# Two PSUM banks emptied by one instruction, merged log sums, factored table fixes and a new order, in a chunked recurrence with an FFT block

## The chip, the cores and the metric

One core of one Trainium2 chip. The metric is the device time of one execution in microseconds (us), as the median of several runs. Every run lists its span on the core and the mean clock that was granted to TensorE (1.0 is full). A run counts as fast when it lies within 1.5% of the fastest run of the same kernel; only fast runs are compared. The engines are called PE (TensorE), DVE (VectorE), ACT (ScalarE) and POOL (GpSimd).

## The reference, cut to what matters

```python
def _attn_ref(r, k, v, w, a, b):            # B, H, S, D = 4, 8, 768, 40, all fp32
    for t in range(S):
        y[:, :, t] = einsum('bhd,bhde->bhe', rt, state)
        Sa = einsum('bhde,bhe->bhd', state, at)
        state = state * wt[:, :, None, :] - einsum('bhd,bhe->bhde', Sa, bt) \
                + einsum('bhd,bhe->bhde', vt, kt)
    return y

def _moe_ref(x, w_ch1, w_ch2):              # x: 4 x 768 x 320
    u = x + np.real(np.fft.fft(np.fft.fft(x, axis=1), axis=2))
    un = (u - mean(u)) / sqrt(var(u) + 1e-6)
    return u + np.maximum(un @ w_ch1, 0.0) @ w_ch2      # 320 -> 1280 -> 320
```

## The kernel before

The recurrence is cut into 24 chunks of 128 steps (6 for each of 4 batches). Each chunk has a part that can be prepared ahead ("prep": running sums of log w on PE, exponentials on ACT, scalings of the inputs, transposes, and three masked products A, N, RV for each head) and a part that needs the state ("chain": several small products, a fourth masked product M, the output y and the new state). After six chunks a batch goes through the Fourier tables, the layer norm and the two dense layers ("post"). For all this there is no scheduler at run time: every operation has a number and one implementation for each engine that may do it, and a long recorded text says in which order, and on which engine, each is issued. The letters are P for PE, A for ACT, D for DVE, G for POOL, S for a DMA and W for a filler matmul that only keeps PE busy.

```python
CODE = "ABC...xyz0123456789+-"
ENGINES = dict(zip("PADGSW", ("PE", "ACT", "DVE", "POOL", "SP", "WARM")))
ORDER = ("AQDASDARDACGBFSBLAAdSAbSAAGATGAHDAUGCZGCaGCbDAcSAgSCeDCgDCpDChDCdDAFDAeS" ...)   # cut
SLOTS = ("ABDCBABCAACBABBAABABCDBFHEAADACAAAFEDABCEFHCFHANLJOIBBBCABBBCAFDEGCHEADG" ...)   # cut: the buffer of each
WIDE = set()
...
    ps = Pool("ps", [psum.tile([128, 512], FP32, tag=f"ps{i}", name=f"ps{i}") for i in range(8)])
...
    op({"DVE": (0.35, lambda: nc.vector.tensor_scalar_mul(nsu16, su16, -1.0))}, w=[NSU], r=[SU])   # the negated mask
```

The product of a chunk for eight heads is written as two halves, even heads in one PSUM bank and odd heads in another. Each half leaves PSUM through a masked eviction: either DVE multiplies by a triangular mask, or ACT copies and then POOL (or DVE) masks in place. `masked` could already do both halves at once, but was not asked to.

```python
    def halves(wide):
        if wide:
            p = PSB(lambda t_: t_.rearrange("p (e q t) -> p e q t", e=2, q=NP), 2)
            return [p], [lambda: p()[:, 0], lambda: p()[:, 1]]
        p2 = [PSB(qv) for _ in range(2)]
        return p2, p2

    def masked(dst, p2, neg=False):
        n_ = 2 // len(p2)                        # 1: a half of 512 columns; 2: both, 1024
        ...
        for e in range(2 // n_):
            o = op({"DVE": (cD(512 * n_), ... nc.vector.tensor_tensor(d_(), all_(p2[e]()), mask, Alu.mult)),
                    "ACT": (cA(512 * n_), ... nc.scalar.activation(d_(), all_(p2[e]()), Act.Copy, scale=...))}, ...)
            op({"POOL": (..., ... nc.gpsimd.affine_select(out=d_(), in_=d_(), compare_op=Alu.is_gt, ...)),
                "DVE": (..., ... nc.vector.tensor_tensor(d_(), d_(), mask2, Alu.mult))}, skip=o, ...)
```

The two other places that the change touches, the sums of the logs and the last fix of the Fourier tables:

```python
        def sums():
            o_ = hd(cum())
            mm(o_, ut16, hi()[:, :, :D], True)
            mm(o_, ut16, low()[:, :, :D], False)
        op({"PE": (cP(2, 320), sums)}, w=[cum["c"]], r=[logw, low, UT], kind="cum")
        if not last:
            def totals():                        # 9 small matmuls into the same bank
                ...
            op({"PE": (0.23, totals)}, w=[cum["t"]], r=[cum["c"], logw, low, ONE, ID, OFF], kind="wl")
...
        def last():
            r_ = DM // 2 - 128
            nc.vector.tensor_scalar_mul(cd[r_:r_ + 1, 3], cd[r_:r_ + 1, 3], 0.5)
            nc.vector.tensor_copy(cd[0:64, 4], cd[0:64, 3])
            nc.vector.tensor_scalar_mul(cd[64:128, 4], cd[64:128, 3], -1.0)
```

Of the kernel before, what the change touches and what calls it, by code (L numbers as in the profile page):

```python
# [12 lines left out]
FP32 = mybir.dt.float32  # L13
# [9 lines left out]
def order_of(text):  # L23
# [6 lines left out]
ORDER = ("AQDASDARDACGBFSBLAAdSAbSAAGATGAHDAUGCZGCaGCbDAcSAgSCeDCgDCpDChDCdDAFDAeSBMGBRPAEDBvSCiAAhABNPCqDCcD"  # L30
    "CfDCsDAiDC-WC-WC-WAnPAoAAfSAjPAmAABGADGBOPAtDBQACrABKSApDB1AAqDE-WE-WEvWAxPAuPAyPArDBISDKSCmDCnDAzA"
    "AsAB2DAIGCoABXAAPGAvPAkPBSAB3PAwDCtDA7PBHSA2PAlAA3ABwSBcPBGSBJSBxSA+DA5DB0SCjGA8AB7PB8AA0PB4PB6AA4D"
    "B5ADQACkDCyPAMGBySBzSA1DBVDFxWBAPBZPBUDCzDA9DBbPC0PEPSC1DD-WDMWC2PDRGAKGDSPBTDClABDABBABEGALDDTPBYP"
    "CuAC3DC8PBdDBaDC4PC5PC6DBWGBePBlPAJGB+GBgPBfDANGC7DDDPC9DBjDDEAAWGB9GCCPCFPBmDBhDDWPBoDDNSDOSDMSDPS"
    "DLSCBGCGPD0PD1PCHDFUSEQSBPADVAD2AEVAB-GCDPC+PCEDFVSDBDDUAD3PD4DCKPCLDC-ADXABqPCPPBrACSDCAGCIPCJDD5P"
    "D6AAVGEWGEXPDbGGXSEUSESSCNDCQDDjPEAPDcAEBADkAD7PD8PD9DERSEYPDaGD+DDePDhPEZABCGDFPEaADAGCUPFaAAZGDZG"
    "DgPDiAAXGCXDAOGD-AAGGDYGBsGCVDECPDGPDHDEdGDdPEbPE5PEHPE6PBtABuGEDDDfDEFDEcAE7ADvPDwAE8PFbGDqPDlPFcP"
    "DyAE9DDtADuGDoDDmDDrDEhAFdAEJPE+PFePE-AEIAGdAEfGFAPEKPEiPFBPFFPELPETSFGAKJSFCDFDDAaDFEAEjPEeGFZSEgG"
    "FXSFgGEMDEkDGeGF8PEmPElPFHPFKDFIDF9PHcSFWSFYSDJGDxGEnAC-WCcWEvPEwDDzGF+AEoPF-PFMPGADEyDCwDEqPFfAEpA"
    "E0PFiDEtDGfPGBPErAFkAEsGFOPGgPGCAFNAGiAGDPFPPGIPGEPHiAGJAFpPGFDGGDE3DFmPFlPFhGFoPFqDGHGFjGFQPGjPFRD"  # L40
    "EOGE1DHBPFrPHjGHCPGZSFnAFtPFuDFwDKPAGaSGnGHgSGYSLJSFsAHDAGKPHEPHFDGPPHkPGcSGhAGkAGmGHoPF3PGNDHGPGLA"
    "F4DGQAF6DHHAHdSFyPHIPF1AHJPHNPHOAHeSHfSHKDGMGDIGGpAGtPGrPGRPGlGGbSFSGHhSHLDHMGF2GFzDGSPGTPGqPKOSKKS"
    "KNSKMSLNSGUDGuPGvDHPPHQDHSDIGPIHPGsAHnAIIAHtAHUPHlPHmAIJPIKDGWGG3PHqGKQGGyPHpAHVAH1PILPHrGLPAHWPG1A"
    "KRPHXPHYPH2DGzDKSPGoAG6DHsGIMAINPKUAIOAG4DHZDHyPGwPGxDKVDG2GKxPIPPISDHwPKyAENGLQGIQDKLSHuAMMSLOSHaG"
    "FTGLRPHzPIUPHvPHxDKbAIVPKTALKSH0ALSPLTAKaAKcSIWPLMSKzPG8PIXDK0DH3PH4DG9DK1PK2AH6AH8PH9DK7PKXGAYGKZG"
    "IbGGVGIfGKWAH-AK8ACvDHbDKePK3PKdPKfAIeDLaANPSLLSCxDKYGLVDIaGIBPICDK4PLUAIEDK5DIgPIhPIjAIlAKgPIiPKhA"
    "KiPK6AG-DInAIoAKjDK9PK+DMSAKnPKqAItPKlDLAAIAGIZGH7GLbGIuDLxPLyPIkGLXGImGLZGLBGIpPIqDIrDLWALYGMTGKsP"
    "LzAIxPLEPL0PKvAKtAI9PLePIsAL1DL2PJDPLdPKoAIyDIvDI5PIzDL3AIwAI+DL4PL5PL6DLFPLfAJEAL9PL+AI0DMOSLgPLhD"
    "JFPI1PJHPJIAJGAL-PMAALGDL7DI2DKuGIYGLnPLiPKpGMNSMPSLcSMQSNRSLoALCPMUPMVPMBGLpGLDAL8GLqAMWAI3DI4AMXA"
    "KrGI6DMCDLjDMGPI7DJbPJLPM0PM1PMHPJXPM2ANQSKwGLlAJMDJcAMYDNVAMZAJYAJJPM3PI-DJZPJAAM4DOQSNUSNSSMIPJTP"  # L50
    "I8AMJDJKDMcGM5PM6AMEPLsPJmPJUDMFDMRSNTSMLGNWGJnAJRPJqPLtDOTSJrALmGJaDJoPNAPNBANXPM7PM8PM9DPTSJpAJVP"
    "NCPMbGMjPLvAJSAORSMkAOWAMaDMhPMgPNFDM+DM-AMdGNYAIcGJWDNDDMiDNZDJuPJ+PN1PMKGJ8POXGJ9AJvAJ-AJ6PN2PN3D"
    "MqPMlPN8PLrGMrAOYPOZPOSSNJPN4PNaAMmAObAMtDNdGLwDOaANeAMeANbGJ7DJ4PNcGNKPNLPN5DN6PIdGMoDNMDJBAN7AJwP"
    "NHPNIAJ5AJxANhPNiPNfDNjDNkPOBPPZAN9PN+DOCDNlAPaGJ2POVSMfSJPPJ0PJQAOcDMnGOgGNrPN-DJ3DNsDJNPJyPNuAOdA"
    "JOANmPNpAOAGMsGODPOEDOlPO4PO5PJsPPbPOGAOeDNnAOkPOfDPcPOnPJzAO6AOoAOmDOKPO7POHGO8DOLPOMPOIPO9PJtANvG"
    "J1DONDNNGOPGNqGOiGNoGOpPOuPPdAPeAO+AO-PPAPPEPPFAJCAOsDPfDOJDOxDPBDPCDJdPJeDPDDKDPKEDOqAOUSOhANgSOvD"
    "NOGP7PKGPKHDOrGP8PS4SR4SPGPP9APJDPHAS+ANwPMvPMwANxAMyDLIGP+PSgPP-DPWSR+APIGJgPQAPQBAShANzDS-GTAPPLP"
    "LHGTBPPUSPXSOjSMxDQCPPNPPOPPMAPjDNyDJhDR-DPVSQDAQJPPPPPQDQKPSiPSjDQEPQFDQHDKAPPRGPSGPkDKBDOzPSkPPYS"
    "PhGTDAPgAPiGSlAO2DPlAQLPQMDTEDSAPSmPQODJjPPqPSEDJkDO0DTFATCAPnPPoPPrAPpASFAQNGOOGSnPSqPSoDSrDQQPQUA"
    "PsPPvDSsPPxPP0DStDSvDQPPQSDR8SR9SSKGSJGSDAPtAPyDR6SSHGQRPR7SSIGQWASPPSQDR5SPmSSGGSpGSNPSMPSOAP2PQTG"  # L60
    "PuGP3DT7SSLSQYPQZDUBAQXGQgPQhDTgPP5AQaDThPTiASBPSWPSCASRPS5SSbPSXASZAScASSDQcPTjPQiDQVGUCGUDPQdDSUA"
    "S7SS6SQkPQoPTkDTGGTMPQbAQeDUEPSeATlPTnPTIGTmAQsPQfDQpDQyPQ0PQzDTNPToPQjAQtDQ1ATHGQ2PSxPSVGSaGTsPTPP"
    "Q3DSyAQ+PQ6PTODSYGJfSTpDV-STqDTrGVBSTQAS9SQ7AQ4PRKPQ-AQlDUFAQqDS8SKCSUjPTtAQmDQuDUkPRAPTuPUlAJlSJiS"
    "T+STKGSdGTxDTJGQvDRLAUmPQrDUnDRGPQ5AQnARHATvATwGRBARIPRJDREPRCPRFAUoPRXPTzPUpASfGSzPRDDT0ARVPRZPRYD"
    "P6GS0PU+SVEAUvPUGAQ8PQ9AULGRWDVFGRaDKISKFSUwDS1DRdPT9ST8SUHDReAUxPU0DUyAUzGUIATWPTZATRPTUAUJGTXDUKD"
    "UqPUrPRtPT1PVGPVHARlPRmATSAT-STLSVDSUMAT2PT3PT4DUsDWCSVASUQPUPPURARhPUSPTTGVOARiAVCSU-SWDSUASRSPXCS"
    "WASVIDRuDUtDTbPUTDWFAUZPZnSTcDUUPUcDWBSRjPU4PT5GTeDRkDVJAUaDUXATVGTaGWGGUuGVMGXDSU5PU6PVkPT6GVlPVmA"
    "WHPVKDWKAWPDRMPQwAVnPVLGUNGVNGQxARTDUVDRrPVQPRsAVRPRfPUOSVTPVSAVrPWIPWJAVPSS2GS3GXHSXFSWESVoDVpPU7D"
    "WLDVqAVUARNDXIARPPRQDVaPVVPRgAUYGWNGVwPVsPVYDVxDWUPXJGWMAVdAWOGWTPWVAVtDU2PRbPRcAVbAWnPRnPU3DVuDVWD"
    "RoDVvGanSXESWWPRpPWXARqAWoPVyPUePV1AU9GV2GUhAWpDWYPWqPUfDWZDWrDXKPRvPWsPVzDV5PV6PV7PRwDWbAWQGWcGXLP"  # L70
    "WuPVeGZtAWtAWvPV8DWwDWdPWxDVfPViAXNAWzPXMAWeDW0DWyAU8GVcGV9GR1PXQGXqPXrPVjGatAV+GXsAW6PaPPXODXPAWgD"
    "VgDXRDW1PaQAWRAXtPXuDW4DRyPauGZuGR2DW2AW7AXSGXvPXwAavPayAXZPV3ParSZoSXGSV4AXxPZvPZyAXaDXyDaRPaSDXTA"
    "awPXzPX2ARzDXXPXWPUiGW8PXUGW3GX0DW9PX3GW+PW-DXBDX4PXYAaTPaUAXAGX5PX6PX7DX9DX8DRxSZqSXgPXbPZwPZzDXjD"
    "Z3GZ1GXhAXcAZxAaZPaVPaWPaxAaXDazDaoSa1DaqSWSSaaAZpSX+PWiPabPaeDbsSbqSZ0AWlAa0AZ2GacDYBAYCGYAPXeDYFA"
    "bwAWjDXdGX-PYDAaYAZ+PZ-AZ8PZ7PZ9DbPPYHPYIDXVSbQPbRAXlPasSR3SXoAYJDcwSROSapSaAPaDAaBAYKARUSR0Sa3GXiG"
    "bSPXmAbTDYPPYQDYLPYGGYEGbUPYbPYMDagPYRDbVAa4GYXPbxGYcDbWPaFPRRSZrSWmGahAaIAa5GaGAbXPbbPYSDaiPYNDYOA"
    "YhPa7Pa8Pa9AbYDYTPbcDbZDXpGa2Ga+PYUDYlPajPa-AYmAaCGbaGbyPbzPb0AYjPYYDYiDbdPakDbgAYkDbeDbAPbFPbGDb2D"
    "bBDbDAaEGZ4GctScSPaJGaHGcTPcUAb1AczAbhGZsSZ5GYpPbrSbuSYzPcVPcWDY1PYrPcXPb3AYqAcuScYAYsAY2AYxPYvPYwA"
    "YdDbtScZPcePYnPcaPbIDY5PcvSYZDbEGa6SXnGc0GamGcbDYyAbkPYaAYoAccDYeAYVDb5GcBPblPcCAb4GY3PY4AbmPbnDYtP"
    "ZIPc1PY0AcfAcdGb6GY6DZJDYuDb-PdTPb+PdUPc2AbiPcADdVAYfAc5DZ6ScgPcjAYgAbvSc7GbKPbNDbLAb8AchAdWPdXDY+P"  # L80
    "b7GalGc3DdYPdZAaKPY-DboGciGcDPcySZAScxSaLAcGAbjDdaPdbPdcDcEDddDdfPdgAZBPcIPbMGYWAaNAdhPcHDc-PZEPcLD"
    "c4AcJAc6DZGPdAPdBAZHAc9DY7PdiDZFDdeDdCPduPc8AdvPY8DdkDZKPdwAdDAZCDb9SZaPZbAZQPZRAZLDaMGcKGdxPdyDcNP"
    "cQAdEPaODcRGcODdJPdMDdKDdFAdzPd0AZWPclPZXAdHAcmDdGGZOPZcPd1Pd2Pd3DdIGdoPd6Pc+Sd4DZUPd5DZPAd7AZdAckG"
    "dpPcnPeJPdqPeKPdOPd8PZVDdmPeLDdrDeMPdPAeNDdsGcoPdQGd9AZMPcpPdnAd+GbpGeOPePAZSPeBPd-DdRDZNDeQPeRDZYP"
    "dtGeDPeEPcqDcrGcsGeCAeFPeGDeSPeXPeYPZZAeVDeIGeTDZTAZkPeHGZlDeZPeaDebDedPeePecDegPehPefPeiPelDejAenA"
    "H-WHkWexPeyDetPepPeuDekAeoGemAe9PezDeqDe0AevDe5PZhPe1PewAerDesDfFPfHPfDPe+De6De2De7DfGAfEAe3DZePZfD"
    "e-DfIAZmSfJPfXPfYAfADfRPfPPfQDfbPZiDfqPfrDe4Ae8AfmPfoPfLPfZPfnDfpAfBAfcDfKAfaAfNPfOAf6PfyPf2PfMAf0P"
    "fsPfSAfTPfUAfzDftDf7Df4Pf5Df8Pf9DfVPf+PfwPfuPfWDfdPf1Af3Af-AfCAfxAfvDgDPgAPY9SgGPfjPgBDfgPZDSgEDfeD"
    "ZjSZgSgFSffSgCSfkDgHDflSgISfhDfiS")
SLOTS = ("ABDCBABCAACBABBAABABCDBFHEAADACAAAFEDABCEFHCFHANLJOIBBBCABBBCAFDEGCHEADGGMPRSQBACGBCCCCGHEFHIAHFBFA"  # L90
    "AABEABHAAAAGFBFCKBEACDCABDDDEAAAEHADBAECDACGCCDBBBBBCDBFGTGLJNKAABAADAABBBBDBCEFEFCGACHABBCCCAAEFED"
    "EFHRMSPBBABBBACCCFDCGDHFDEAHDHCDAGABABBHECADIDTCJFDCBACBCHAABAHGBIEGFAHDAGABBCBCBAAGGCDCQBGKAICAABD"
    "FBBBBABFBCAGHFBGFBECDABBBHAGAAGHFACBACGDCEBFAGAEAEAEAAGEFFGABDHHBHDFBEEFCHBGFBCHBAONQPHLABBAADDCCAE"
# [20 lines left out]

# [147 lines left out]
def kernel(  # L262
# [15 lines left out]
    DM = H * D  # L278
# [603 lines left out]
```

## Time and profile before

| | before |
|---|---|
| median of 3 runs | 247.58 us (247.32 to 247.58) |
| run that was profiled | 248.41 us, of which 246.7 us span, clock 1.0 |
| masked evictions | 112 halves on DVE, 80 on ACT |
| ends of the four batches' last chunks | 61.0, 116.9, 169.7, 216.2 us |

The prediction shows the engine rows, the stretches and the chain. The costliest groups of the page that the change is about (engine, operation, output from inputs, shapes, count, then busy us and mean ns of one, then the idle time ahead of them):

```profile
L448 POOL TENSOR_SCALAR_AFFINE_SELECT pr<-pr 128x512 bf16<-128x512 bf16 x58 | 37.0, 647 | 9.1 <-ACT pr L155 9.0
L155 ACT ACTIVATE pr<-ps 128x512 bf16<-128x512 f32 x65 | 37.4, 609 | 3.0 <-PE ps L155 1.7
...
L155 DVE TENSOR_TENSOR pr<-ps,su 128x512 bf16<-128x512 f32 x50 | 33.3, 681 | 1.1 <-PE ps L155 0.5
```

The two evictions wait little (1.1 and 3.0 us in all for their groups): they are limited by their engines, not by what feeds them. POOL's masks wait 9.1 us, nearly all of it for ACT's copies. The lines of DVE's timeline have start, duration, instruction.

### The profile page before, as it was taken

The page shows a single profiled execution, that of the slowest core. Times are in us where ns is not written, and L with a number is a line of the kernel's source. Part 1 is how long each engine was busy: PE and PEld are TensorE (multiplying, and loading weights), DVE is VectorE, ACT ScalarE, POOL GpSimd, SP SyncE. Part 2 cuts the span into 40 slices and gives each one's busy share as a digit, 9 for nine tenths or more (in the row PEclk, how much of TensorE's full clock was granted, in tenths as well). Part 3 has the DMA queues.
Part 4 walks back from the last instruction along what each step waited for, and adds up shares of the span by engine and source line. Part 5 has one row for each costly group of instructions (what it writes and reads, how often), then busy time and mean ns, then how long its engine had stood idle before and what let it go on. Part 6 is the DMA issues. An engine that isn't in the chain of part 4 may idle for free.

```text
span 246.7 us, 9106 instructions
## 1 busy us (share of the span) xinstructions
PE 226.6 (92%) x3649; PEld 173.0 (70%) x3649; DVE 219.3 (89%) x471; ACT 184.7 (75%) x420; POOL 155.6 (63%) x274
## 2 busy tenths in 40 slices
PE   2797899799798999999999999999999999999994
PEld 1365777588676777777886877877777778876672
DVE  5889999999999998999999898999998999869623
ACT  2489898787699999845698977787999987545610
POOL 7309689699857786654794898686879723700000
PEclk9999999999999999999999999999999999999999
DMA  7999999997989987995989999999989151020104
GB/s 126 178 179 160 178 171 162 157 153 129 157 156 175 178 134 106 182 160 103 160 165 231 176 159 161 169 177 145 260 145 150 20 110 34 3 81 0 56 0 159
DMA packets 171834, 33.94 MB, mean 138 GB/s; under 512 B 167120, under 2 KB 171472, under 8 KB 171792
## 3 DMA queue, kind: packets, MB, share of 16 engines
q1 hardware_dynamic: 170112, 31.73, 72.6%
q0 software_dynamic: 1680, 1.64, 4.6%
q8 instruction: 28, 0.46, 0.8%
q14 instruction: 14, 0.11, 0.1%
HBM read 26.87 MB, written 3.93 MB: 125 GB/s over the span
## 4 chain that ended last, share of the span: by engine, by line
PE 60%; DVE 25%; ACT 7%; issue 5%; POOL 2%; DVEq 0%; ACTq 0%; POOLq 0%
PE ps L155 60%; DVE pr L155 7%; DVE nat L155 3%; ACT pr L155 2%; DVE h L155 2%; DVE m L155 2%; DVE xb L155 2%; DVE xs L155 2%; DVE pm L155 1%; DVE ar L155 1%; DVE s L155 1%; DVE kb L155 1%; POOL pr L448 1%; DVE wp L155 1%; DVE cd L155 1%
## 5 line engine op out<-in xcount | busy, mean ns | idle before, releaser
L155 PE MATMUL ps<-unT,w1sb 128*128 128x384 bf16 x240 | 45.8, 326 | 0.3 <-DVE xb L155 0.3
L448 POOL TENSOR_SCALAR_AFFINE_SELECT pr<-pr 128x512 bf16<-128x512 bf16 x58 | 37.0, 647 | 9.1 <-ACT pr L155 9.0
L155 ACT ACTIVATE pr<-ps 128x512 bf16<-128x512 f32 x65 | 37.4, 609 | 3.0 <-PE ps L155 1.7
L155 PEld LDWEIGHTS <-nat 128*128 128x128 bf16 x512 | 30.3, 99 | 8.7 <-DVE nat L155 2.3
L155 PE MATMUL ps<-w2sb,h 128*128 128x320 bf16 x240 | 35.5, 299 | 0.0
L155 PEld LDWEIGHTS <-pr 128*128 128x128 bf16 x768 | 29.0, 96 | 8.3 <-issue 2.1
L155 DVE TENSOR_TENSOR pr<-ps,su 128x512 bf16<-128x512 f32 x50 | 33.3, 681 | 1.1 <-PE ps L155 0.5
L155 PE MATMUL ps<-ident,nat 128*128 128x128 bf16 x352 | 31.1, 223 | 2.3 <-DVE pr L155 1.3
L455 POOL TENSOR_TENSOR nat<-in,rw 128x320 bf16<-128x320 f32 x36 | 31.3, 874 | 2.4 <-ACT rw L155 1.6
L155 ACT ACTIVATE h<-ps 128x384 bf16<-128x384 f32 x53 | 24.6, 502 | 6.1 <-PE ps L155 5.9
L155 PEld LDWEIGHTS <-w1sb 128*128 128x128 bf16 x240 | 21.0, 98 | 10.9 <-issue 0.4
L155 PEld LDWEIGHTS <-h 128*128 128x128 bf16 x240 | 22.7, 98 | 8.5 <-issue 0.2
L635 POOL TENSOR_TENSOR pm<-xb 128x161 bf16<-128x161 f32 x40 | 19.9, 510 | 8.8 <-DVE xb L155 8.8
L468 POOL TENSOR_TENSOR low<-logw 128x320 f16<-128x320 f32 x21 | 15.8, 755 | 14.4 <-ACT logw L155 12.2
L155 DVE TENSOR_TENSOR m<-ps,su 128x512 bf16<-128x512 f32 x33 | 21.9, 680 | 0.9 <-PE ps L155 0.8
L155 DVE TENSOR_TENSOR pr<-ps,nsu 128x512 bf16<-128x512 f32 x29 | 19.5, 679 | 0.4 <-PE ps L155 0.3
L155 PE MATMUL ps<-ar,kb 64*128 64x128 bf16 x384 | 17.9, 221 | 1.3 <-DVE kb L155 0.7
L155 PE MATMUL ps<-xs,pr 128*128 128x40 bf16 x384 | 17.3, 180 | 1.7 <-DVE xs L155 0.8
L155 DVE SCALAR_TENSOR_TENSOR xb<-ps,bst,xb 128x320 f32<-128x320 f32 x24 | 12.8, 543 | 6.4 <-PE ps L155 6.4
L455 POOL TENSOR_TENSOR nat<-in,wp 128x320 bf16<-128x320 f32 x18 | 15.8, 880 | 4.0 <-ACT wp L155 3.0
L155 PE MATMUL ps<-nat,pr 128*128 128x40 bf16 x384 | 17.2, 180 | 0.2
L155 DVE TENSOR_SCALAR h<-ps 128x384 bf16<-128x384 f32 x27 | 14.4, 549 | 3.2 <-PE ps L155 3.2
(143 smaller groups left out, 585.8 us busy)
## 6 DMA issues: line engine op xcount, KB each, us to landing
in<-in_w_dram SPq DMA_DIRECT2D x24, 160.0 KB, 4.0
in<-in_a_dram SPq DMA_DIRECT2D x24, 160.0 KB, 4.0
in<-in_k_dram SPq DMA_DIRECT2D x24, 160.0 KB, 3.9
in<-in_r_dram SPq DMA_DIRECT2D x24, 160.0 KB, 3.9
in<-in_b_dram SPq DMA_DIRECT2D x24, 160.0 KB, 3.8
in<-in_v_dram SPq DMA_DIRECT2D x24, 160.0 KB, 4.0
out_dram<-xb SPq DMA_DIRECT2D x24, 160.0 KB, 3.0
w2sb<-in_moe_w_ch_dram POOLq DMA_DIRECT2D x2, 400.0 KB, 5.5
```

The source lines that it names most:

```text
L155: i = f(*args, **kwargs)
L448: op({"POOL": (0.035 + 0.563 * n_, lambda d_=d_: nc.gpsimd.affine_select(out=d_(), in_=d_(), compare_op=Alu.is_gt, fill=0.0, base=0, patte ...
L455: return {"POOL": (0.82, lambda: nc.gpsimd.tensor_tensor(dst(), x_(), s_(), Alu.mult)), "DVE": (cD(320), lambda: nc.vector.tensor_tensor(d ...
L468: op({"POOL": (0.68, lambda: nc.gpsimd.tensor_tensor(low()[:, :, :D], lg(), hi()[:, :, :D], Alu.subtract)), "DVE": (cD(320), lambda: nc.ve ...
L635: op({"POOL": (0.46, lambda a_=a_, f_=f_: nc.gpsimd.tensor_tensor(*a_(), f_)), "DVE": (cD(161), lambda a_=a_, f_=f_: nc.vector.tensor_tens ...
```

## The change

The intent: a DVE instruction that reads PSUM has a fixed part, so one instruction over two banks should cost less than two. PSUM becomes four pairs of banks, and all 24 chunks take the wide form. Besides, the totals of the logs are made in the same operation as the sums, ahead of them; the table fix becomes two full-height multiplications by a factor for each row; and the whole order was recorded anew, with other engines for many operations.

```diff
-ORDER = ("AQDASDARDACGBFSBLAAdSAbSAAGATGAHDAUGCZGCaGCbDAcSAgSCeDCgDCpDChDCdDAFDAeS" ...
+ORDER = ("HWDAQDAUDAEDAHDAVDAIDAMGACGAAGAbSADGARDA+SBEAAfSCEGCFGCJDCIDCRDCGDABGAPD" ...      (cut)
-WIDE = set()
+WIDE = {0, 1, 2, 3, 4, 5, 6, 7, 8, 9, 10, 11, 12, 13, 14, 15, 16, 17, 18, 19, 20, 21, 22, 23}
@@
-    ps = Pool("ps", [psum.tile([128, 512], FP32, tag=f"ps{i}", name=f"ps{i}") for i in range(8)])
+    banks = [psum.tile([128, 1024], FP32, tag=f"ps{i}", name=f"ps{i}") for i in range(4)]
+    ps = Pool("ps", [banks[i // 2][:, i % 2 * 512:(i % 2 + 1) * 512] for i in range(8)], banks)
@@
         def sums():
+            if not last:
+                o_ = cum()[:, DM:DM + 2 * NP].rearrange("p (q e) -> p q e", e=2)
+                for q in range(NP):
+                    for n_, x_ in enumerate((hi(), low())):
+                        mm(o_[:, q], x_[:, 2 * q:2 * q + 2, :].rearrange("t h d -> t (h d)"), ones2, q + n_ == 0)
+                mm(cum()[:, DM:DM + 2 * NP], ident16, off_d.rearrange("p q e -> p (q e)"), False)
             o_ = hd(cum())
-            mm(o_, ut16, hi()[:, :, :D], True)
+            mm(o_, ut16, hi()[:, :, :D], last)
             mm(o_, ut16, low()[:, :, :D], False)
-            op({"PE": (0.23, totals)}, w=[cum["t"]], r=[cum["c"], logw, low, ONE, ID, OFF], kind="wl")   (its body cut)
@@
+            nc.gpsimd.memset(pn()[:, 8:10], 1.0)
+            nc.gpsimd.memset(pn()[DM // 2 - 128:DM // 2 - 127, 8:9], 0.5)
+            nc.gpsimd.memset(pn()[64:128, 9:10], -1.0)
@@
-        def last():                                                                                 (its body cut)
-        op({"DVE": (0.8, last)}, w=[CD], lock=("DVE",), kind="tab")
+        op({"DVE": (0.22, lambda: nc.vector.tensor_scalar_mul(cd[:, 3], cd[:, 3], pn()[:, 8:9]))}, w=[CD], r=[pn], ...)
+        op({"DVE": (0.22, lambda: nc.vector.tensor_scalar_mul(cd[:, 4], cd[:, 3], pn()[:, 9:10]))}, w=[CD], r=[pn], ...)
```

Cut besides: the rest of the two order texts, some estimated durations that only the search for an order uses, and a form of transpose by DMA that the change provides but no chunk uses.

## The prediction

> **What bounds the kernel now.** I read four views in this order: the page's engine rows, the busy time by stretches, the chain of work that ended last, and the timeline of VectorE. The engine rows come first:
>
> ```profile
> span 246.7 us, 9106 instructions
> PE 226.6 (92%) x3649; PEld 173.0 (70%) x3649; DVE 219.3 (89%) x471; ACT 184.7 (75%) x420; POOL 155.6 (63%) x274
> PE ps L155 60%; DVE pr L155 7%; DVE nat L155 3%; ACT pr L155 2%; DVE h L155 2%; DVE m L155 2%; DVE xb L155 2%; DVE xs L155 2%; DVE pm L155 1%; DVE ar L155 1%; DVE s L155 1%; DVE kb L155 1%; POOL pr L448 1%; DVE wp L155 1%; DVE cd L155 1%
> ```
>
> Two engines look full, TensorE (PE) and VectorE (DVE), and the chain passes 60% of its time through PE and 25% through DVE. By stretches (busy us of each engine in 12.3 us):
>
> ```profile
> 37.00:49.30 12.30, 10.42 (x212) 8.32 (x208) 12.23 (x24) 10.43 (x24) 10.04 (x16) 1.00 0.92 159
> 49.30:61.70 12.40, 11.81 (x276) 10.09 (x275) 12.37 (x25) 10.10 (x25) 11.87 (x21) 1.00 0.84 141
> ...
> 111.00:123.40 12.40, 12.40 (x223) 10.25 (x219) 12.18 (x26) 7.47 (x17) 7.81 (x14) 1.00 0.76 132
> 123.40:135.70 12.30, 12.30 (x192) 9.31 (x191) 12.02 (x34) 11.56 (x27) 8.61 (x16) 1.00 0.93 198
> ...
> 222.00:234.40 12.40, 12.40 (x92) 7.97 (x90) 9.86 (x26) 7.33 (x18) 0.00 (x0) 1.00 0.08 28
> ```
>
> The columns are PE, PEld, DVE, ACT, POOL, clock, DMA. In the first batch (to about 61 us) DVE has no gap at all while PE has some. Later both are full, and the last 30 us belong to PE alone. The chain says the same: from 35 to 66 us nearly every step is DVE, then come long PE pieces such as
>
> ```profile
> 103.61 34.91 PE ps L155 x553
> 183.01 16.08 PE ps L155 x260
> 202.10 41.28 PE ps L155 x469
> ```
>
> A busy PE is not a full PE, so I measured its real need: how far apart equal matmuls start when nothing holds them. 40 columns: 25 ns; 80: 35; 128: 55 (two row halves of 64 together: 55 a pair); 320: 136; 384: 162. Times the counts this is 198 us of the 246.7. For DVE I did the same, because consecutive instructions overlap:
>
> ```profile
> 50.12 1.28 DVE L155 TENSOR_TENSOR pr<-ps,su 128x512 bf16<-128x512 f32 x2
> 51.32 0.49 DVE L155 TENSOR_TENSOR ps<-ps,s 128x320 f32<-128x320 f32 x1
> 63.13 0.23 DVE L155 TENSOR_SCALAR cd<-cd 128x320 bf16<-128x320 bf16 x1
> 63.28 1.67 DVE L155 TENSOR_TENSOR pm<-xb 128x161 bf16<-128x161 f32 x2
> 64.98 0.56 DVE L155 TENSOR_SCALAR cd<-cd 1x320 bf16<-1x320 bf16 x1
> 65.58 0.41 DVE L155 COPY cd<-cd 64x320 bf16<-64x320 bf16 x1
> 66.00 0.71 DVE L155 TENSOR_SCALAR cd<-cd 64x320 bf16<-64x320 bf16 x1
> 66.74 0.49 DVE L155 TENSOR_TENSOR wp<-ps,logw 128x320 f32<-128x320 f32 x1
> ```
>
> Two 512-wide evictions start at 50.12 and the next instruction at 51.32: 0.60 us each, although the groups give one a mean of 0.68. The last 0.08 us of each lies under the next one. This is the main thing to see here, because the naive saving from the durations would be twice too large.
>
> **What the Trainium skill says.** "Advanced Engine Details and Errata", section The Read-Write Bubble, says that memory latency shows between instructions and not within a tile, advises tiles of 512 or 1024 elements, and says that one instruction may read several PSUM banks. That is the intent of this change. The trace agrees in kind, but the bubble is small here: 320 fp32 columns from PSUM are spaced 0.398 us, 512 are 0.598, so 1.04 ns a column and only 0.065 us fixed. "VectorE: DVE Perf Modes", in its errata section, gives 120 cycles fixed (0.125 us) for PSUM to SBUF; where instructions stand back to back the trace shows half of that. "Perfetto Trace Analysis", Identifying the Most-Contended Engine, says that matmul busy time is a bad measure of how near PE is to its limit; the 226.6 us against the 198 worked out above agree. "PSUM — Partial Sum Buffer", PSUM bank collisions raise a hardware error, says that two engines may not touch one bank at a time; so a wide eviction has to have both banks finished and to itself. No run shows this yet.
>
> **The change part by part.** The order in which each engine's instructions stand can be built for both kernels, so counts are exact; durations are spacings from the trace.
>
> Wide products. 24 chunks have 4 products of two halves, 192 halves. Before, DVE evicts 112 and ACT 80; ACT's are then masked by POOL (73) or DVE (7). After, DVE takes 54 pairs and ACT 42 (37 masked by POOL, 5 by DVE). A wide DVE eviction is 0.065 + 1024/960 = 1.132 us. DVE: 112 x 0.598 = 67.0 becomes 54 x 1.132 = 61.1, so -5.9. ACT: 80 x 0.477 = 38.2; its 1024-column copies of kb are spaced 0.908, so 42 x 0.905 = 38.0: nothing, because it now has a larger share. POOL: 128 columns 0.243, 512 are 0.587, so 1024 about 1.05; 73 x 0.587 = 42.9 becomes 38.7, -4.2. DVE's own masks: 7 x 0.344 becomes 5 x 0.61, +0.6.
>
> Table fixes. The three instructions take from 64.98 to 66.74, 1.76 us in a stretch in which DVE sets the pace. Two full-height ones, spaced about 0.15 to 0.23 like the one at 63.13, replace them: -1.4. POOL gets three tiny memsets at the start, 0.1 us each.
>
> Sums and totals in one go. The same 9 small matmuls (25 ns each, 0.23 us) now stand ahead of the two wide ones and share their bank's one owner. No PE work goes; one semaphore does in each of 20 chunks; the exp for rw starts 0.2 us later. I count it as zero.
>
> New order. DVE hands off 7 scalings (4.1 us), 4 input casts (2.0), 3 relus (1.5), 3 state casts (1.0), 2 folds (1.1), 2 vt copies and 1 low part (1.1) and 1 unT copy (0.3), and takes 4 zz copies (2.2), 2 un (1.0), 2 ar, 1 kb, 1 snT, 1 sn (2.1), an angle step (0.6) and about 1.5 us of memsets, some of which fill its idle time before 3.9 us. Net -3.7. POOL takes 7 scalings and 8 casts (+9.5), which eats what it saved; ACT falls by 3 to 4 us. PE loses 5 to 8 warm-up matmuls, about 1 us.
>
> Sum: DVE -5.9 + 0.6 - 1.4 - 3.7 = -10.4 (a row-by-row sum of the whole order gives -11.5: 218.7 to 207.2). PE falls 1.1.
>
> Not all of this reaches the end. I summed both orders up to the DVE instruction that writes the last chunk's output of each batch (in the trace at 61.0, 116.9, 169.7 and 216.2 us). Stage 1: DVE 56.2 to 54.3, PE 34.8 to 34.1; DVE sets the pace, so 61.0 becomes 59.1. Stage 2, 55.9 us: DVE 52.3 to 47.6, PE 45.6 to 44.6; after that DVE is only 3 us above PE, so I pass on two thirds of 4.7: 52.7. Stage 3, 52.8 us: DVE 50.0 to 48.8, PE 49.6 to 48.9; both bind, -0.9: 51.9. Stage 4, 46.5 us: DVE 42.6 to 39.0, but PE 40.7 to 40.8; the stage is 5.8 above PE's need, of which I give back 1.2: 45.3. Tail, 30.5 us, PE alone: 27.3 to 28.5, so 31.7. Total 240.7 of span against 246.7; the timed median lies 0.9 above the span, so about 241.5 us.
>
> **The rivals.** First, PE is the bound and what DVE saves turns into waiting. For it: the 34.91, 16.08 and 41.28 us chain pieces, and stages 3 and 4, in which PE's need is within 3 to 6 us of the time. Against: stage 1 and much of stage 2 have 10 to 25 us of PE slack. Then only stage 1 and the table fix count, and the time is 244 to 245.5. Second, PSUM becomes the wait. A pair needs two neighbouring banks of eight, and they come free only after 1.13 us on DVE or 0.9 on ACT, where two engines could empty the halves side by side in 0.6 (as at 104.20, when ACT and DVE both start one). 96 pairs x 2 banks x 0.5 us is about 100 bank-us out of 8 x 247, some 5%. If PE stalls for it, perhaps half of the gain goes: 244 to 246. Third, POOL. It gets 9.5 us of scalings and casts which feed the transposes, in pieces of 0.84 us that were 0.57 on DVE, and its masks become 1.05 us long; if the next chunks' operands come late, 245 or more. Its 63% speaks against. Fourth, all of DVE's saving reaches the end of stage 4, because DVE stays as full as it was: 216.2 - 11.4 + 31.7 = 236.5, so 237.4 timed.
>
> **Range and chances.** The middle estimate is 241.5. The fourth rival gives the lower edge, 236.5, and the second and third the upper one, 246.5. The line for 2% faster is 242.6, only 1.1 above the estimate, and two rivals lie beyond it, so faster gets 0.6 and within 2% gets 0.38. Slower needs +5 us with less work on every full engine: 0.02.
>
> **What would show it.** Right: the 1024-wide evictions spaced about 1.13 us on DVE and 0.9 on ACT; DVE busy at 207 to 210 us and ACT at 180 to 183; the two table instructions under 0.5 us together; the last output of the first batch at about 59 us and of the second near 112; the last 30 us unchanged or slightly longer. The estimate is wrong if DVE shows gaps ended by PE in stages 1 and 2 (PE or PSUM binds earlier than I thought), if PE's waits on DVE or ACT grow from the few us of now, if POOL's spacing of wide masks is far above 1.05, or if DVE busy falls by 10 us and the span by less than 3.

## More of the kernel before

```profile
7.12 0.18 DVE L155 TENSOR_SCALAR nsu<-su 128x128 bf16<-128x128 bf16 x1
7.22 0.48 DVE L155 SCALAR_TENSOR_TENSOR h<-h,h 128x320 f32<-128x320 f32 x1
```

The negated mask (`nsu`) is made early, in 0.10 us from its start to the start of the next instruction, and a 320-column step of the table angles (`h<-h,h`) in 0.40 us.

## The result

| | before | after |
|---|---|---|
| median | 247.48 us (247.32 to 247.58, 4 runs) | 244.3 us (243.6 to 244.55, 4 runs) |
| ratio, with 95% interval | 1 | 0.9868 (0.9844 to 0.9891) |
| granted clock | 1.0 (profiled run) | 0.986, 0.986, 0.993, 0.993 |

A ratio here is the mean time of one kernel's fast runs over the mean of the other's of the same rounds, so it is not quite the ratio of the medians. The kernel is 1.3% faster, which counts as "within 2%". The time lies inside the range of the prediction and 2.8 us above its middle; the likelier class that it named, faster by over 2%, did not come.

From the page of the profiled execution after: the span, the engines, the chain by line, and the same groups as above.

```profile
span 242.8 us, 8954 instructions
...
PE 223.3 (92%) x3642; PEld 172.9 (71%) x3642; DVE 210.2 (87%) x407; ACT 182.0 (75%) x379; POOL 156.5 (64%) x247
...
PE ps L152 63%; DVE h L152 4%; DVE pr L152 3%; DVE m L152 2%; SPq L416 2%; DMA in<-in_v_dram 1%; ACT pr L152 1%; DVE s L152 1%; SPq L752 1%; DVE xb L152 1%; DVE ps L152 1%; DVE ar L152 1%; DVE nat L152 1%; DVE xs L152 1%; ACT un L152 1%
...
L152 DVE TENSOR_TENSOR pr<-ps,su 128x1024 bf16<-128x1024 f32 x31 | 37.4, 1216 | 1.4 <-PE ps L152 0.6
...
L152 ACT ACTIVATE pr<-ps 128x1024 bf16<-128x1024 f32 x33 | 33.4, 1028 | 3.8 <-PE ps L152 3.7
...
L447 POOL TENSOR_SCALAR_AFFINE_SELECT pr<-pr 128x1024 bf16<-128x1024 bf16 x28 | 30.6, 1096 | 4.9 <-ACT pr L152 4.7
```

DVE lost 9.1 us of busy time, about what was forecast, and the span lost 3.9. The chain has moved from DVE to PE, as intended: the evictions (`pr`) were 7% of it on DVE and are 3%. One entry is new near the top, "DVE h": most of it the steps that make the table angles in the first 14 us.

The stretches of 12 us (columns as in the prediction: PE, PEld, DVE, ACT, POOL, clock, DMA share, GB/s):

```profile
12.10:24.30 12.20, 9.14 (x121) 6.28 (x119) 10.41 (x16) 9.59 (x18) 6.46 (x12) 0.79 1.14 170
24.30:36.40 12.10, 10.35 (x202) 8.52 (x199) 11.00 (x19) 10.99 (x22) 9.13 (x14) 0.93 1.04 176
...
218.50:230.70 12.20, 12.20 (x91) 7.91 (x90) 8.28 (x21) 6.95 (x18) 0.00 (x0) 1.00 0.16 55
```

The first stretch is the odd one: PE, DVE and POOL all have gaps, nobody is full, and the clock fell to 0.79. The last belongs to PE alone, as before. And four pieces of the chain (start, length, what):

```profile
15.21 1.25 DVE nsu L152
...
22.50 9.26 PE ps L152 x161
...
102.52 53.48 PE ps L152 x858
...
188.60 50.87 PE ps L152 x631
```

The long PE pieces in batches 2 to 4 are what the forecast expects of a kernel whose DVE has become lighter. The first two pieces are not: the negated mask, a 128 by 128 multiplication that took 0.10 us before, is on the path with 1.25 us, and a PE piece of 9 us follows whose matmuls run at half clock up to 26.0 us (the clock record of this profile shows half from 19.2 to 26.0).

To see where the time went, I took the DVE instruction that writes the last output of each batch, in every profile, and the spans between them. The last three columns are from experiments that follow.

| us | before | forecast | after | after, second profile (e12) | pairs split again (e1) | negated mask moved (e5) |
|---|---|---|---|---|---|---|
| stage 1 | 61.0 | 59.1 | 62.1 | 60.8 | 61.7 | 59.8 |
| stage 2 | 55.9 | 52.7 | 52.1 | 52.2 | 52.4 | 52.2 |
| stage 3 | 52.8 | 51.9 | 52.6 | 53.3 | 53.1 | 52.6 |
| stage 4 | 46.5 | 45.3 | 44.3 | 44.3 | 46.4 | 44.3 |
| tail | 30.5 | 31.7 | 31.7 | 31.7 | 31.7 | 31.7 |
| span | 246.7 | 240.7 | 242.8 | 242.3 | 245.3 | 240.6 |

After misses the forecast by 3.0 us in stage 1 and by at most 1.0 us, with both signs, anywhere else. In the second profile, taken at full clock, stage 1 misses by 1.7 and stage 3 by 1.4. So the main question is the first 60 us. DVE's timeline there:

```profile
10.23 0.99 DVE L152 TENSOR_SCALAR h<-h 128x320 f32<-128x320 f32 x1
11.15 2.08 DVE L152 SCALAR_TENSOR_TENSOR h<-h,h 128x320 f32<-128x320 f32 x2
...
15.14 1.33 DVE L152 TENSOR_SCALAR nsu<-su 128x128 bf16<-128x128 bf16 x1
15.91 0.68 DVE L152 COPY kb<-ps 128x1024 bf16<-128x1024 bf16 x1
16.52 2.34 DVE L152 TENSOR_TENSOR pr<-ps,su 128x1024 bf16<-128x1024 f32 x2
```

Nothing here waits for data, yet the two `h<-h,h` steps take 1.00 us each from start to start instead of 0.40, and the mask holds up the next instruction for 0.77 us instead of 0.10. POOL's timeline of the same time says what ran beside them:

```profile
10.16 0.88 POOL L454 TENSOR_TENSOR nat<-in,rw 128x320 bf16<-128x320 f32 x1 [3.84 <-ACT nat L152]
11.01 0.80 POOL L467 TENSOR_TENSOR low<-logw 128x320 f16<-128x320 f32 x1
...
15.08 0.86 POOL L454 TENSOR_TENSOR nat<-in,wp 128x320 bf16<-128x320 f32 x1
```

POOL's multiplication runs from 15.08 to 15.94; the mask is issued at 15.14, and the next DVE instruction starts at 15.91. The two wide evictions that follow, which read PSUM, keep their 1.13 us. The Trainium skill, "SBUF — State Buffer", section SBUF: two separate sides, says that GpSimd and VectorE share one pair of SBUF ports as an exclusive lock, that whichever instruction starts first has it to its end, and that a VectorE instruction asks for it in a two-port mode or with two SBUF inputs. The trace agrees as far as it goes: the mask (one SBUF input, bf16) and `h<-h,h` (two SBUF inputs) are held, the PSUM readers are not. That the mask runs in a two-port mode is not something that the trace shows. In the kernel before, the mask (7.12 us) and the 320-column `h<-h,h` stood where POOL did nothing of the kind. But it was not free of this: a 386-column `h<-h` at 4.56 us, beside a multiplication of POOL, took 0.81 us there (0.28 in after), and an `h<-it,sm` at 6.30 took 0.82 (0.38 alone).

### The profile page after: what moved, and what is told of

The parts are those of the page before. It is cut to its first block, busy times and chain, and to the rows that moved or that the text cites. A ratio compares the mean times of both kernels' runs of the same rounds, so it can differ in the third digit from the quotient of the medians.

```text
span 242.8 us, 8954 instructions
## 1 busy us (share of the span) xinstructions
PE 223.3 (92%) x3642; PEld 172.9 (71%) x3642; DVE 210.2 (87%) x407; ACT 182.0 (75%) x379; POOL 156.5 (64%) x247
## 4 chain that ended last, share of the span: by engine, by line
PE 63%; DVE 18%; ACT 7%; issue 4%; SPq 3%; DMA 1%; POOL 1%; DVEq 0%; POOLq 0%
PE ps L152 63%; DVE h L152 4%; DVE pr L152 3%; DVE m L152 2%; SPq L416 2%; DMA in<-in_v_dram 1%; ACT pr L152 1%; DVE s L152 1%; SPq L752 1%; DVE xb L152 1%; DVE ps L152 1%; DVE ar L152 1%; DVE nat L152 1%; DVE xs L152 1%; ACT un L152 1%
## 5 line engine op out<-in xcount | busy, mean ns | idle before, releaser
L454 POOL TENSOR_TENSOR nat<-in,rw 128x320 bf16<-128x320 f32 x41 | 35.7, 877 | 9.6 <-ACT rw L152 4.0
L152 DVE TENSOR_TENSOR pr<-ps,su 128x1024 bf16<-128x1024 f32 x31 | 37.4, 1216 | 1.4 <-PE ps L152 0.6
L152 ACT ACTIVATE pr<-ps 128x1024 bf16<-128x1024 f32 x33 | 33.4, 1028 | 3.8 <-PE ps L152 3.7
L447 POOL TENSOR_SCALAR_AFFINE_SELECT pr<-pr 128x1024 bf16<-128x1024 bf16 x28 | 30.6, 1096 | 4.9 <-ACT pr L152 4.7
L152 ACT ACTIVATE h<-ps 128x384 bf16<-128x384 f32 x56 | 26.5, 498 | 5.9 <-PE ps L152 5.6
L647 POOL TENSOR_TENSOR pm<-xb 128x161 bf16<-128x161 f32 x42 | 21.6, 530 | 7.0 <-DVE xb L152 6.9
L454 POOL TENSOR_TENSOR nat<-in,wp 128x320 bf16<-128x320 f32 x20 | 17.6, 880 | 8.7 <-ACT wp L152 8.5
L152 DVE TENSOR_TENSOR m<-ps,su 128x1024 bf16<-128x1024 f32 x15 | 18.2, 1218 | 1.5 <-PE ps L152 1.4
L152 PEld LDWEIGHTS <-kb 64*128 64x128 bf16 x384 | 11.9, 95 | 7.1 <-issue 2.2
L152 ACT ACTIVATE sn<-ps 128x320 bf16<-128x320 f32 x22 | 9.8, 444 | 8.5 <-PE ps L152 7.9
```

The source lines that it names most:

```text
L152: i = f(*args, **kwargs)
L447: op({"POOL": (0.035 + 0.563 * n_, lambda d_=d_: nc.gpsimd.affine_select(out=d_(), in_=d_(), compare_op=Alu.is_gt, fill=0.0, base=0, patte ...
L454: return {"POOL": (0.82, lambda: nc.gpsimd.tensor_tensor(dst(), x_(), s_(), Alu.mult)), "DVE": (cD(320), lambda: nc.vector.tensor_tensor(d ...
L647: op({"POOL": (0.46, lambda a_=a_, f_=f_: nc.gpsimd.tensor_tensor(*a_(), f_)), "DVE": (0.33, lambda a_=a_, f_=f_: nc.vector.tensor_tensor( ...
```

## The experiments

The theories. The first (its second half is theory L): the wide eviction gives what was forecast, and the start-up gives back some of it, because the new order puts table steps and the negated mask of DVE beside two-input work of POOL. Rivals: the wide form itself costs time elsewhere because each pair of banks is held longer (bank holding); the loss is the clock of TensorE, which in the profile of after fell to half at 19.2 us, as theory C has it because PE had little to do before; and the new order alone is the gain or the loss (theory O). There were three sittings, each with its own runs of the kernel before: medians 247.39, 247.42 and 247.6 us. Ratios are against these. All results were correct.

### e1: wide pairs split again, in the new order

```diff
-WIDE = {0, 1, 2, 3, ... 23}
+WIDE = set()
 ORDER: every wide eviction and its mask become two halves, one behind the other, on the same engine; all else as after
```

> The changed kernel, its order kept, with each wide eviction and each wide mask cut into its two 512-column halves, one after the other on the same engine. Theory of the prediction: VectorE pays 54 x 0.065 = 3.5 us more, ScalarE 42 x 0.04 = 1.6, GpSimd 37 x 0.11 = 4.1; VectorE busy rises from 210 to about 213.5 us, and some two thirds of it reach the end: 246 to 247 us against 244.3. Rival (holding two banks for 1.13 us costs PE as much as the saved fixed time gives): the halves come free sooner, PE waits less, and the time stays within 0.5 us of 244.3 or falls below it.

Measured: 247.38 us (246.63 to 248.53), ratio 1.000 (0.9973 to 1.0027). The page:

```profile
span 245.3 us, 9091 instructions
...
PE 221.9 (90%) x3642; PEld 171.2 (70%) x3642; DVE 215.3 (88%) x466; ACT 184.3 (75%) x421; POOL 161.1 (66%) x284
```

Splitting costs 3.1 us (247.38 against 244.3), where 1.7 to 2.7 were expected: so in this order the wide form is worth the whole gain, and bank holding falls as a net loss. DVE rose by 5.1 us to 215.3, more than the 3.5 expected. Spacings went back to 0.598 on DVE, 0.477 on ACT and 0.587 on POOL. The other finding is as important: with the new order, the new table fix and the merged sums, but without the wide form, the kernel takes what the kernel before takes, although its DVE is busy for 4.0 us less (215.3 against 219.3). This order was recorded for pairs, so it says nothing of an order made for halves. Of the gain from the wide form the table of stages shows 0.9 us in stage 1 and 2.1 in stage 4, when the second profile of after is taken, which ran at the same full clock.

### e2: more fillers in the thin stretch

```diff
 ORDER of after: + 3 W, + 2 W, + 2 W, + 2 W  among the operations issued at 12 to 19 us
```

> The changed kernel with 9 more filler matmuls of 504 columns, put on free PSUM banks in PE's gaps between 12 and 19 us. Theory C (the granted clock fell to half from 19.2 to 26.0 us because PE had too little to do before, and this ate the gain of the first batch): granted clock 1.0 in all runs, VectorE's idle time of some 3 us between 21 and 33 us shrinks to under 1, the first batch's last output comes at about 60 us in place of 62.1, time 242.0 to 242.8. Rival L (VectorE's stretched instructions behind GpSimd in the first 16 us are the loss, not the clock): clock 1.0 but the time stays at 243.8 to 244.5.

Measured: 244.41 us (243.33 to 244.44), ratio 0.9862 (0.9839 to 0.9884). The same stretches:

```profile
12.10:24.30 12.20, 10.84 (x145) 6.79 (x142) 11.24 (x17) 10.49 (x20) 6.82 (x13) 1.00 1.07 172
24.30:36.40 12.10, 10.12 (x192) 7.89 (x192) 11.03 (x20) 11.20 (x22) 9.87 (x15) 0.91 1.01 174
```

The clock is whole where it had been 0.79, a fall came later in the profiled run (from 34.2 us), and the time is that of after. The one run that kept clock 1.0 took 244.35 us. Theory C alone is out. Whether the fillers kept the clock up is not shown, because the second profile of after (e12) is at full clock in these stretches without them.

### e3: fewer fillers in the kernel before

```diff
 ORDER of before: - E-W E-W EvW, - FxW, - D-W DMW, - C-W CcW   (8 of the fillers between 10 and 35 us)
```

> The kernel before with its 8 filler matmuls between 10 and 35 us taken out, the first three kept. Theory C: the granted clock falls for one or two stretches of 6.8 us (mean 0.97 to 0.99) and the time rises from 247.5 to 248.5 to 249.5. Rival L: the time stays within 0.4 us of 247.5 whatever the clock does, because VectorE sets the pace there.

Measured: 248.34 us (247.62 to 249.43), ratio 1.0033 (1.0008 to 1.0058). Of six runs one had 0.991 and the others 0.999 or 1.0, and those spread over the whole range. So 0.8 us were lost, mostly without a fall in the clock that the runs show. This is more than theory L allowed (0.4) and less than theory C forecast (1.0 or more); it decides nothing for or against C.

### e4: the old table fix in the new kernel

```diff
-        op(... nc.vector.tensor_scalar_mul(cd[:, 3], cd[:, 3], pn()[:, 8:9]) ...)
-        op(... nc.vector.tensor_scalar_mul(cd[:, 4], cd[:, 3], pn()[:, 9:10]) ...)
+        def last():  ...  (the three instructions of before)
```

> The changed kernel with the three old table-fix instructions at the place of the first of the two new ones (36.5 us). Theory of the prediction: they take about 1.2 us more on VectorE in the stretch where it sets the pace, so 245.2 to 245.7 us against 244.3. Rival: at 36 us VectorE has slack behind PE, and the time stays within 0.4 us of 244.3.

Measured: 245.16 us (243.96 to 246.3), ratio 0.9903 (0.9876 to 0.9929), so 0.9 us above after, with intervals that just overlap. In after, the two new instructions take 0.41 and 0.26 us from start to start, 0.67 together, where the prediction said under 0.5:

```profile
36.50 0.48 DVE L152 TENSOR_SCALAR cd<-cd,sm 128x320 bf16<-128x320 bf16 x1
...
61.98 0.29 DVE L152 TENSOR_SCALAR cd<-cd,sm 128x320 bf16<-128x320 bf16 x1
```

### e8: the new table fix alone, in the kernel before

```diff
+            nc.gpsimd.memset(pn()[:, 8:10], 1.0)          (and the two rows of factors)
-        op({"DVE": (0.8, last)}, ...)
+        op(... cd[:, 3] by pn()[:, 8:9] ...), op(... cd[:, 4] = cd[:, 3] by pn()[:, 9:10] ...), in its place
```

> The kernel before with the table fix by per-row factors alone (two instructions in place of three, at about 65 us). Theory of the prediction: VectorE sets the pace there, 1.4 us less: 246.0 to 246.6 against 247.4. Rival (the stretch after 66 us waits for ScalarE and PE): within 0.4 us of 247.4.

Measured: 246.88 us (246.35 to 247.92), ratio 0.9984 (0.9968 to 1.0): 0.4 us, where 0.8 to 1.4 were expected (1.4 in the prediction); the interval reaches to nothing at all. The timeline has the reason in one line:

```profile
64.74 1.12 DVE L155 TENSOR_SCALAR cd<-cd,sm 128x320 bf16<-128x320 bf16 x2
```

The next instruction starts at 65.78, so the two take 1.04 us together in this place, and not 0.3 to 0.5. The fix saves 0.7 us of DVE here, and the rest of the forecast was never there. Reading e4 and e8 together, the fix is worth 0.4 to 0.9 us, each in its own order and with a wide interval.

### e5: the negated mask made earlier

```diff
 ORDER of after: the operation AFD (nsu = -1 * su) moves from place 73 to place 18, ahead of the table steps
```

> The changed kernel with one instruction moved: the negated mask (0.10 us by itself), which stood at 15.14 us on VectorE and was held there for 0.77 us while GpSimd ran a two-input multiply, now stands before the table steps, at about 4.1 us, where VectorE has nothing to do. Theory L (table steps and the mask, held behind GpSimd in the first 16 us, ate the gain of the first batch): the first evictions come some 0.6 us earlier, 243.3 to 243.8 us against 244.3. Rival (the first batch is paced by something else, such as PE's answers at 21 to 33 us): within 0.3 us of 244.3.

Measured: 242.58 us (242.36 to 242.97), ratio 0.9808 (0.9795 to 0.9821), clock 1.0 in all five runs. This is 0.7 us better than even theory L expected. Its ratio's interval lies wholly below that of after. With e6 (242.66) this is the fastest of the kernels here; whether it is faster than before by 2% stays unclear, as the interval holds 0.98. The work of every engine is that of after; only one instruction has another place. DVE's timeline:

```profile
3.92 0.13 DVE L152 TENSOR_SCALAR nsu<-su 128x128 bf16<-128x128 bf16 x1
...
10.24 0.32 DVE L152 TENSOR_SCALAR h<-h 128x320 f32<-128x320 f32 x1
...
15.55 2.35 DVE L152 TENSOR_TENSOR pr<-ps,su 128x1024 bf16<-128x1024 f32 x2
```

and POOL's:

```profile
10.27 1.01 POOL L454 TENSOR_TENSOR nat<-in,rw 128x320 bf16<-128x320 f32 x1 [3.95 <-ACT nat L152]
...
15.24 0.86 POOL L454 TENSOR_TENSOR nat<-in,wp 128x320 bf16<-128x320 f32 x1
```

The mask costs its 0.1 us again, and the first evictions start at 15.55 instead of 16.52. POOL's multiplication at 15.24 now lies beside the evictions and holds up none of them. The lines at 10.2 us are a small lesson of their own. In after, POOL started at 10.16, DVE's `h<-h` at 10.23, and it took 0.99 us. Here DVE started at 10.24, POOL only at 10.27, and now DVE takes its 0.32 and POOL's becomes the longer one, 1.01. Who comes first has the ports.

### e6 and e9: the same with more fillers, and with fewer

```diff
 e6, ORDER of e5: + 11 W between 12 and 35 us
 e9, ORDER of e5: - 5 of the W of the first 20 us
```

> The same with the 9 filler matmuls of the earlier run and 2 more at about 32 us, so that the clock should fall neither at 19 nor at 34 us. Theory C in its second form (the fillers helped, but the fall only moved to 34 us): granted clock 1.0 in most runs and 242.0 to 243.0 us. Theory L alone: as the run with the mask moved, 243.3 to 243.8. If neither matters: 244.0 to 244.5.

> The changed kernel with the negated mask moved early (242.6 us, granted clock 1.0 in all its runs), and its five filler matmuls between 11 and 16 us taken out. Theory C (a fall of the granted clock near 20 us costs about 1 us, so of the 1.7 us that the moved mask gave about half came from the clock staying full): the clock falls in most runs (mean below 0.995) and the time is 243.3 to 244.3 us. Theory L alone: within 0.4 us of 242.6 whether the clock falls or not.

Measured: e6 242.66 us (242.41 to 243.28), ratio 0.9811 (0.9798 to 0.9823), clock 0.999 to 1.0: against e5 the fillers add nothing. The number lies in the range that was named for theory C, but only because e5 itself came out below its forecast. e9 243.15 us (243.11 to 243.98), ratio 0.9826 (0.9805 to 0.9846). That is 0.55 us above e5 by the medians, just outside what theory L allowed (243.0) and below what theory C named (243.3), so neither was met. At clock 1.0 one of its runs took 243.11 us; at 0.986, 0.984 and 0.986 the others took 243.15, 243.15 and 243.98. So in these four runs the time does not follow the clock clearly. Where in the kernel the clock fell in the last three isn't on record: only the first was profiled.

### e10: the table steps later as well

```diff
 ORDER of e5: the three 320-column table steps CXD, CVD, CYD move behind the first scalings
```

> The changed kernel with the negated mask moved early and three table steps of VectorE (at 10.2 to 12.5 us, stretched there to 2.3 us behind GpSimd) put after the two scalings of the first chunk. Theory L (the first chunk's operands wait behind table steps): the first evictions come about 1 us earlier than 15.55 us and the time falls to 241.4 to 242.2 us against 242.6. Rival (the sines on ScalarE then come late and its later work with them): 242.6 or more.

Measured: 244.0 us (243.87 to 245.72), ratio 0.9866 (0.9842 to 0.9890), 1.4 us slower than e5. A miss. The collisions only moved: the scalings, which have two SBUF inputs too, now took 0.87 and 0.93 us from start to start (0.40 alone), the table steps still were held, and the first eviction began at 16.93 us instead of 15.55.

### e11: sums and totals apart again

```diff
 e5 with sums() and totals() as two operations, as in the kernel before; the totals behind the sums in the order
```

> The changed kernel with the negated mask moved early (242.6 us), with sums and totals of the logs as two operations again, the totals right after the sums as in the kernel before. Theory of the prediction: PE does the same matmuls, so nothing changes: within 0.4 us of 242.6. Rival: rw can start 0.2 us earlier in 20 chunks, so it is 0.5 us or more faster.

Measured: 243.56 us (242.94 to 244.06), ratio 0.9836 (0.9815 to 0.9857): 1.0 us in the medians and 0.7 in the ratios (0.0028 of 247.5) above e5, with intervals that overlap by a little. The merged form, with the totals ahead of the sums, seems worth something like 0.7 us, where I had counted it as zero. By the profiles the difference lies in stage 1, which ends at 60.7 us against 59.8 in e5.

### e7: the wide form in the old order

```diff
 before, with banks and WIDE as in after; ORDER: each pair is evicted in one instruction where its first half stood (56 on DVE, 40 on ACT); PSUM slots given anew
```

> The kernel before in its own order with the 96 products leaving two banks in one instruction: 56 pairs on VectorE, 40 on ScalarE (before: 112 and 80 halves), each at the place of its first half, PSUM banks given out anew. Theory W (the wide eviction itself is worth some 3 us in any order): VectorE busy falls by 3.6 us, 244.0 to 245.5 us. Rival O (it pays only in an order laid out for it, because 46 of the 96 pairs were emptied side by side by two engines, and because pairs must wait for two neighbouring banks): 247 to 250 us.

Measured: 281.34 us (278.62 to 285.21), ratio 1.1331 (1.129 to 1.1371), from the four fast runs of six; the profiled run was a slow one. DVE's busy time fell by 3 us to 216.2, and yet every engine had gaps, such as this one of PE's weight loads, which have 8.3 us of idle time ahead of this group in before:

```profile
L150 PEld LDWEIGHTS <-pr 128*128 128x128 bf16 x768 | 30.0, 97 | 18.0 <-issue 10.8
```

Far outside anything that I expected. In before, 46 of the 96 pairs had their halves evicted by two engines, and my places for the wide ones and my choice of banks are not tuned. So this doesn't measure the wide form in the old order; it shows that this simple way of keeping an order recorded for halves fails by 34 us. Whether a better choice of places and banks would save it was not tried. The worth of the new order as the wide form's companion is thus not a number that I have.

### e12: after once more

> The changed kernel as it is, in the same rounds as the other three, so that they can be compared on one chip: 244.3 us, within 0.4. If it is nearer to 243 here, what the moved mask gave is smaller than 1.7 us.

Measured in the sitting of e9 to e11: 244.17 us (243.81 to 244.62), ratio 0.9860 (0.9840 to 0.9879). Clocks 1.0, 0.991, 0.993 and 0.993 went with 243.98, 244.62, 243.81 and 244.35. After is reproduced, its run at full clock is no faster than the rest, and the same steps are held in its profile.

The two profiles of after are of one program and differ in the clock. First a DVE line of the first profile, then the stretch, the first evictions and the same DVE instruction in the second:

```profile
23.95 0.49 DVE L152 TENSOR_TENSOR s<-ps,wt 128x320 f32<-128x320 f32 x1 [1.51 <-PE ps L152]
...
12.10:24.30 12.20, 8.31 (x135) 5.84 (x133) 11.24 (x17) 10.49 (x20) 6.81 (x13) 1.00 1.13 163
...
16.52 2.34 DVE L152 TENSOR_TENSOR pr<-ps,su 128x1024 bf16<-128x1024 f32 x2
...
22.95 0.49 DVE L152 TENSOR_TENSOR s<-ps,wt 128x320 f32<-128x320 f32 x1 [0.96 <-PE ps L152]
```

Both start the first evictions at 16.52 us. In the first profile, with the clock at half from 19.2 to 26.0, the later instruction comes 1.0 us later, after a longer wait for PE, and stage 1 ends 1.3 us later. So within stage 1 the fallen clock did cost about 1.3 us in that profile. Only 0.5 of it is left in the span, because the second profile lost 0.7 in stage 3, which I can't explain.

The 1.6 us between after and e5 (0.0060 and 0.0052 of 247.5 give 1.5 and 1.3 by the ratios) are real, and the clock is not the main part of them: the two runs at full clock with the mask late took 243.98 (e12) and 244.35 (e2), the slowest of e5 242.97. By the profiles at full clock (e12 and e5) the spans differ by 1.7 us: 1.0 in stage 1 and 0.7 in stage 3.

## Why the prediction was right or wrong

- **The wide eviction: right.** Spacings in after are 1.132 us on DVE, 0.915 on ACT and 1.058 on POOL, against 1.132, 0.905 and 1.05. (A slip in the working: 37 x 1.05 is 38.9 and not 38.7.) Undoing it alone in the new order cost 3.1 us (e1).
- **DVE's busy time: nearly right in sum.** It fell by 9.1 us to 210.2, just outside the 207 to 210 that was named (10.4 to 11.5 less), and the counts of evictions and masks were exact.
- **Stages 2 to 4: right to 1.0 us each in the first profile and to 1.4 in the second, with both signs; the tail exactly** (30.5 and 1.2 more of PE work). That DVE's saving would arrive only in part held: DVE was busy for 4.9 us less in stage 2 and 5.4 less in stage 4, and the stages fell by 3.8 and 2.2. The reason given, PE's need just below, was not tested.
- **Stage 1: the step that failed.** "Stage 1: DVE 56.2 to 54.3 ... DVE sets the pace, so 61.0 becomes 59.1": it became 62.1 (60.8 in the second profile, at full clock). DVE did not become lighter there at all: it is busy for 56.7 us in stage 1 of after and for 56.0 in that of before. That sum took every DVE instruction at the spacing that it has in the kernel before. The new order gave POOL two-input work in the first 16 us and put DVE's SBUF steps beside it: two table steps at 1.00 instead of 0.40 us (+1.2), one `h<-h` at 0.92 instead of about 0.23 (+0.7), the mask at 0.77 instead of 0.10 (+0.7). That is 2.6 us, to be set against about 1.0 for the two steps that were held in before. Moving the mask alone brings stage 1 to 59.8 and the span to 240.6, where the forecast had 240.7; the match is luck, as the table steps of e5 are still held (2.00 us for the two). That the mask's place costs about 1.0 us of stage 1 at the same full clock is shown by e5 against e12; that the held table steps cost anything was argued only, and e10, which moved them, was slower. The other 1.3 us of the first profile's miss came with the fallen clock (e12), which the forecast did not consider.
- **A misread line, and a sign that came.** "In the first batch DVE has no gap at all" is true only from 22 us on: in the first 22 us of before DVE is busy for 17.2, so the start-up had room that the sum took as filled. The prediction also named gaps of DVE ended by PE in stage 1 as a sign of being wrong. They came: 2.6 us after 22 us in the first profile and 1.7 in the second, where before has none.
- **The offset from span to time: 0.8 us too small.** "The timed median lies 0.9 above the span" set the median of one set of runs against the span of another run, a slow-ish one (248.41 us). Within one run the time lies 1.7 us above the span, in before (248.41 and 246.7) as in after (244.55 and 242.8). With 1.7 the same stages would have given 242.4. Put otherwise, the forecast took 6.0 us off the median, although the run that they were worked out on was 0.8 us slower than the median; where that run lost the 0.8 is not known. Of the miss of 2.8 us about 2.1 are span, on balance all of it stage 1, and the rest is this.
- **The new order, "net -3.7": not confirmed as DVE work, and worth nothing as time in e1.** At the prediction's own prices e1 should have 6.5 us less DVE work than before (3.7 for the order, 1.4 for the fix, 1.4 for four evictions fewer and three masks more). It has 4.0 us less busy time, and the time is the same. As the fix and the merged sums seem to be worth about 1 us between them, the new order by itself would be a slight loss; this is a subtraction of small numbers with wide intervals and not a measurement.
- **The table fix, "-1.4": 0.4 to 0.9.** The full-height multiplications are cheap only where nothing holds them.
- **Sums and totals, "I count it as zero": perhaps 0.7 us** (e11), not settled.
- **The rivals.** PSUM as the wait: e1 says that holding pairs costs less than it gives. POOL as the trouble: named, but for the wrong reason. I feared that its operands would come late; what hurt, as far as e5 shows it, was that it ran beside DVE's SBUF steps and held them. What I had put against this rival, POOL's share of 63%, was no argument: a share of busy time doesn't say whom an engine disturbs.

What stays open. The mask was held for 0.67 us too long, and moving it gave about 1.0 us at the first eviction and 1.3 to 1.6 at the end. The 1.0 can be followed: 0.77 for the mask's place, and the rest because the scalings ahead of it fell differently against POOL. At full clock the same 1.0 is there at the end of stage 1 (60.8 and 59.8). The other part, 0.7 us in stage 3 of e12, is not explained. What the clock costs in the end is open too: in stage 1 of one profile it was about 1.3 us, and in whole times e2, e9 and e12 show no gain with the clock whole; an effect of half a microsecond or so can't be ruled out.

## What to carry to other kernels

When you move work to GpSimd, look at which VectorE instructions will then run beside it: here those that read only SBUF took up to two and a half (0.40 to 1.00 us) or nearly eight times (0.10 to 0.77) their time, while those that read PSUM kept theirs. So price an instruction by its neighbours in the new order, not by its duration in the old trace, and put one-off set-up steps where GpSimd is idle, but look again afterwards: in e10 the collisions only moved. An eviction of two banks at once is a sound small gain where both banks are finished together, but the one simple try at keeping the old order (e7) cost 34 us; and take the offset from span to time from one and the same run.

## What the Trainium skill lacked or had wrong

- "VectorE: DVE Perf Modes", the errata section, gives 120 cycles fixed for PSUM to SBUF on VectorE and 172 on ScalarE, besides one a column. As the duration of one instruction this is near: the estimate from that table is 0.66 us for 512 fp32 columns and 1.19 for 1024 on VectorE (measured means 0.681 and 1.216), and 0.57 and 1.00 on ScalarE (0.609 and 1.028). What the table lacks is the price back to back: 0.598 and 1.132 us on VectorE, so 0.065 us fixed and 1.04 ns a column, and 0.477 and 0.915 on ScalarE, from which 0.04 us fixed remain.
- "Perfetto Trace Analysis", the remark on the overhead of each instruction: it gives about 125 ns for DVE and 51 ns for ScalarE on PSUM, and says that the second half of an instruction's latency overlaps the next one. The overlap is right (about 0.08 us on DVE: mean 1.216, spacing 1.132; 0.11 on ACT: 1.028 and 0.915), and ScalarE's figure is near; DVE's is twice the 0.065 us of the runs. What it lacks is the consequence, that a mean in the list of groups overstates the price of an instruction.
- "SBUF — State Buffer", SBUF: two separate sides, has the lock, but what the page measures of it are single operations set against each other, not a kernel. Here a 0.10 us instruction became 0.77, a 0.40 us one 1.00, and moving the one instruction that was held for 0.67 us too long gained 1.3 to 1.6 at the end.
- "PSUM — Partial Sum Buffer" has the rule on collisions but no example of one read over two banks; 96 such reads in each execution, each behind its own product, gave correct results in every run of the wide form.
